# Queries and keys in one transfer of 112 partitions, one row of values, keys and gates, token rows in order of making, list entries of 64 bytes

## The chip, the core and the metric

The program runs on one core of a Trainium2 chip. Its engines are TensorE (PE, with its weight loads PEld), VectorE (DVE), ScalarE (ACT), GpSimd (POOL) and SyncE (SP, which here only issues transfers). Transfers are issued from the queues of SP, ACT and POOL and carried by 16 DMA engines. The metric is the time of one execution on the device in microseconds (us), the median of the runs.

## The reference

Two stages in a row: a recurrent memory with exponential gates over 4 sequences of 8 heads, 768 steps and 40 columns a head, and then a layer of 16 experts, in 4 groups of 4, to which each of the 3072 tokens is routed alone. Cut to what matters:

```python
for t in range(S):                                   # S = 768, B = 4, H = 8, D = 40
    m_new = np.maximum(f_gate[:, :, t] + m, i_gate[:, :, t])
    f_stab = np.exp(f_gate[:, :, t] + m - m_new)
    i_stab = np.exp(i_gate[:, :, t] - m_new)
    m = m_new
    C = f_stab * C + i_stab * outer(vt, kt)
    n = f_stab * n + i_stab * kt
    y[:, :, t] = sigmoid(o_gate[:, :, t]) * (C @ qt) / np.maximum(np.abs(n @ qt), 1.0)
x = y.transpose(0, 2, 1, 3).reshape(B * S, H * D)    # 3072 tokens of 320
g_idx = argmax(x @ w_group); e_idx = argmax(x @ w_expert[g_idx])
out[token] = g_w * e_w * (np.maximum(x @ w1[g, e], 0) @ w2[g, e])   # 320 -> 1024 -> 320
```

## The kernel before

**Attention.** The sequence is cut into 12 chunks of 64 steps, and the 4 sequences into 2 pairs, so that there are 24 units `u`. A unit's 128 partitions are 64 steps of two sequences. `unit(u)` is written out by hand as a row of stages: `scores` (PE, products of keys and queries), `masked` (DVE, `pt`, the scores times the decays `ab`), `carried` (PE, the state of earlier chunks), `state` (PE), `decayed` (POOL), `carried2` (DVE), `values` (PE), `busy` (products that are thrown away), `decay(u + 2)` (PE `aw`, then eight exponentials on ACT, `ab`), `norm`, `state2` (DVE), `keyw(u + 1)` (POOL), `turn(u - 1)`, `norm1`, `rows` and `rows2`. `rows` makes `xn` from the sums and the output gates, `rows2` makes the token rows `x` (on POOL up to unit 19, on DVE after). `turn` copies 64 columns (ACT), stores the rows to the DRAM tensor `x_d`, and turns them on PE (`tp`, then the ACT copy `xT`) for the router. The tile `x` has three buffers.

**Loads.** `unit(u)` starts with `loads(u + 3)`: queries and keys `qk` (four buffers) in two transfers of 48 partitions, at partitions 0 and 64, and `nt` (four buffers), values and keys by row. The output gates come as `sig` for four units at once, and one tanh on ACT (`gate_o`) covers four units.

**Routing.** Every fourth unit, `logits_of` takes four units' `xT` to logits on PE, copies them on ACT (`lT`) and turns them back on PE. `route` is a list of small DVE steps that are put in between the units one at a time (`go_on`): the choice of group and expert, the place of each token in its expert's list (`slot`), and its factor `cb`, which is stored behind its row in `x_d` (columns 384 to 391). `put_id` writes the tokens' numbers into the lists `itab` in DRAM, 128 at a time, by an indirect DMA from POOL. The lists are filled beforehand with the number of a dummy row (`first_tokens`).

**Experts.** When the counts of the first five sixths of the tokens are known, the two fullest experts are picked and their weights loaded. The first 256 tokens of the fullest one (`(0, 0)`) are gathered while the last four units still run, the next 128 (`(0, 1)`) come by the late list `li`, when the last unit's `slot` is written; then come the other 15 experts. Weights are split into a high and a low part (`w1h`, `w1l`, `wsk`, `w2h`, `w2l`: the high parts on ACT, the low parts on DVE), tokens into `xhl`; `psh` and `hh` are the hidden layer, `po` and `y` the output, which an indirect DMA scatters to the tokens' rows. `ix` are list pieces read back, `xg` the gathered rows.

**Order.** Up to unit 21 instructions go out in the order in which they are written. From unit 22 on a scheduler orders them by its own estimates, and each engine and each queue then runs its own in that order. A transfer on SP's queue that has to wait for its data holds up every transfer behind it.

Of the kernel before, what the change touches and what calls it, by code (L numbers as in the profile page):

```python
# [18 lines left out]
P = 128  # L19
# [19 lines left out]
QR = 48  # L39
# [22 lines left out]
def lstm_moe(ctx: ExitStack, tc: tile.TileContext, gates, qkT, nat, og, wcat, w1, w2, cst, out):  # L62
# [7 lines left out]
    itab = dram.tile([NE * NBLK + 1, P], I32, name="itab")  # L70
    itab_flat = itab.rearrange("a (p o) -> (a p) o", o=1)
# [11 lines left out]
    tokid = const.tile([P, NU], I32, name="tokid")  # L83
# [217 lines left out]
    def x_rows(c, p):  # L301
        return [x_d[(NP * p + b) * S + c * L:(NP * p + b) * S + (c + 1) * L] for b in range(2)]

    def turn(u):
        x = st_[u]["x"]
        nc.scalar.copy(x[:, DM:3 * P], x[:, 2 * P:DM])
        done = [nc.sync.dma_start(rows_[:, 0:3 * P], x[halves(b)]) for b, rows_ in enumerate(x_rows(*divmod(u, NP)))]
        if u // 4 == NG - 1:
            no_order("early", *done)
# [30 lines left out]
    def logits_of(c, n):  # L340
# [7 lines left out]
        nc.scalar.copy(lT[0:32 * n], t[0:32 * n])  # L348
        nc.tensor.transpose(out=bank[:, 0:32 * n], in_=lT[0:32 * n], identity=ident[0:32 * n, 0:32 * n])
# [4 lines left out]
    def route(c, b0, b1, bank):  # L354
# [54 lines left out]
        ids.extend((slot[:, b - b0:b - b0 + 1], tokid[:, c * 4 + b:c * 4 + b + 1]) for b in range(b0, b1))  # L409
# [38 lines left out]
    def no_order(key, *some):  # L448

        for ins in some:  # L450
            for o in unordered.setdefault(key, []):
                tc.declare_no_dep(ins.ins, o.ins, reason="distinct rows")
        unordered[key].extend(some)


    def first_rows():
        t = wst.tile([P, 3 * F], F32, name="w1s")
        none, zero = t[:, 0:NE * NBLK].bitcast(I32), t[:, F:F + ROW]
        nc.gpsimd.memset(none, DUMMY)
        nc.gpsimd.memset(zero, 0.0)  # L460
        rt["rows"] = none, zero

    def first_tokens():
        none = rt["rows"][0]
        nc.sync.dma_start(itab[0:NE * NBLK, :].rearrange("(p a) b -> p (a b)", p=P), none)
        nc.sync.dma_start(itab[NE * NBLK:NE * NBLK + 1, :], none[0:1, 0:P])

    def last_rows():
        zero = rt["rows"][1]
        for b in range(B):  # L470
            nc.sync.dma_start(x_d[b * S + S - P:(b + 1) * S, :], zero)
        nc.sync.dma_start(x_d[NTOK:NTOK + 1, :], zero[0:1])
# [127 lines left out]
    def load_ix(r, q=None):  # L600
        nb = len(blocks(CAPS[r]))
        ixs[r] = mxp.tile([P, 3], I32, name="ix", bufs=5)
        t = itab[0:NE * NBLK].rearrange("(e n) p -> e n p", e=NE)
        (q or nc.sync).dma_start(ixs[r][:, 0:nb], t[bass.ds(ereg[r], 1), 0:nb, :].rearrange("o n p -> p (o n)"))
# [4 lines left out]
    def load_x(W, idx, early=False):  # L609
        xg = []  # L610
        for i, m in enumerate(blocks(W)):
            g = mxp.tile([P, ROW], F32, name="xg", bufs=9)
            ins = gather(g, x_d, idx(i, P))
# [66 lines left out]
    def expert(key, W, ws, xg, idx, between=(), then=None, last=None):  # L680
# [65 lines left out]
        for i, m in enumerate(blocks(W)):  # L746
# [27 lines left out]
            done = scatter(y[0:m], idx(i, m))  # L774
# [16 lines left out]
    def ix_of(r):  # L791
        return lambda i, m: ixs[r][0:m, i:i + 1]
# [4 lines left out]
    def unit(u):  # L797
# [5 lines left out]
        if u % 4 == 1 and u // 4 + 1 < NG:  # L803
            load_o(u // 4 + 1)
# [8 lines left out]
        run(carried2, u)  # L813
        go_on()
# [5 lines left out]
        if u % 4 == 1 and 1 < u < NU - 4:  # L820
            logits_of(u // 4 - 1, 4)
        if u == NU - 4:
            logits_of(NG - 2, 3)
# [14 lines left out]
        if u % 4 == 3 and u // 4 + 1 < NG:  # L838
            gate_o(u // 4 + 1)
# [54 lines left out]
    with tc.manual_schedule():  # L894
# [18 lines left out]
        load_o(0)  # L913
# [31 lines left out]
        nc.gpsimd.tensor_copy(tokid, cs[:, C_TOK:C_TOK + NU])  # L945
# [62 lines left out]
    for r in range(NEARLY):  # L1008
        li = mxp.tile([P, 1], I32, name="li", bufs=2)
        nc.sync.dma_start(li, itab_flat[bass.ds(lreg, P), :])  # L1010
        late_ix[r] = lambda i, m, t=li: t[0:m, 0:1]
# [38 lines left out]
    with tc.For_i(0, nv, 1):  # L1050
# [23 lines left out]
        ix = wk2.tile([P, 1], I32, name="ix1")  # L1074
        gather(ix, itab_flat, si)
        g = mxp.tile([P, ROW], F32, name="xg", bufs=9)
        gather(g, x_d, ix)
# [21 lines left out]
        scatter(y, ix)  # L1099
# [5 lines left out]
def _lay(inputs):  # L1105
# [6 lines left out]
    def tr(a):  # L1112
        a = a.reshape(NP, 2, 2, 4, NCH, L, D).transpose(4, 0, 2, 6, 3, 1, 5).reshape(NU, 2, D, 4, P)
        return np.concatenate([a, np.zeros_like(a[:, :, :QR - D])], axis=2)

    qkT = c(np.stack([tr(k), tr(q)], axis=3))
# [8 lines left out]
    nat = c(np.concatenate([vv.reshape(NU, P, DM + H), rows_s(k).reshape(NU, P, DM)], axis=-1))  # L1125
    og = c(rows(o).reshape(NU, P, DM).transpose(1, 0, 2))
# [29 lines left out]
    return {'gates': gates, 'qkT': qkT, 'nat': nat, 'og': og, 'wcat': wcat, 'w1': w1, 'w2': w2, 'cst': cst}  # L1156
# [22 lines left out]
```

## Time and profile before

| | us |
|---|---|
| median of 3 runs | 475.73 |
| lowest, highest | 473.14, 479.25 |
| the profiled execution | 477.46 |
| its span, first to last instruction | 475.4 |

| engine | busy us | share of the span |
|---|---|---|
| PE | 407.7 | 86% |
| PEld | 364.6 | 77% |
| DVE | 284.9 | 60% |
| ACT | 216.5 | 46% |
| POOL | 170.0 | 36% |

The shares are means over two stages with different limits, attention up to some 200 us and experts after it; so the stretches are read apart. A row of a timeline says when an instruction (or several alike in a row, x2) started, how long it took, and in brackets how long its engine had stood idle before it and what ended that. On SP's queue the time is that of issuing the transfer, not of the transfer.

### The profile page before, as it was taken

The page shows a single profiled execution, that of the slowest core. Times are in us where ns is not written, and L with a number is a line of the kernel's source. Part 1 is how long each engine was busy: PE and PEld are TensorE (multiplying, and loading weights), DVE is VectorE, ACT ScalarE, POOL GpSimd, SP SyncE. Part 2 cuts the span into 40 slices and gives each one's busy share as a digit, 9 for nine tenths or more (in the row PEclk, how much of TensorE's full clock was granted, in tenths as well). Part 3 has the DMA queues.
Part 4 walks back from the last instruction along what each step waited for, and adds up shares of the span by engine and source line. Part 5 has one row for each costly group of instructions (what it writes and reads, how often), then busy time and mean ns, then how long its engine had stood idle before and what let it go on. Part 6 is the DMA issues. An engine that isn't in the chain of part 4 may idle for free.

```text
span 475.4 us, 13522 instructions
## 1 busy us (share of the span) xinstructions
PE 407.7 (86%) x5470; PEld 364.6 (77%) x5470; DVE 284.9 (60%) x718; ACT 216.5 (46%) x549; POOL 170.0 (36%) x209
## 2 busy tenths in 40 slices
PE   5667986977854878689399999999999999999995
PEld 3355864665643656568399999999999999999995
DVE  5477465575833777362667475485667677777331
ACT  1524244244413533016077454575565665567421
POOL 4234346354541543230543504432331265133210
PEclk8666698579775755559799999999999999999998
DMA  8933478987399535438589635758665876654300
GB/s 212 238 94 91 112 213 160 237 159 192 70 198 310 71 96 146 92 121 185 124 278 418 216 129 196 254 181 292 215 218 194 288 278 215 223 183 143 147 15 9
DMA packets 30227, 85.74 MB, mean 180 GB/s; under 512 B 12961, under 2 KB 16746, under 8 KB 26580
## 3 DMA queue, kind: packets, MB, share of 16 engines
q1 hardware_dynamic: 24788, 67.63, 50.6%
q0 software_dynamic: 5152, 16.75, 9.9%
q8 instruction: 43, 0.70, 0.7%
q10 hardware_dynamic: 224, 0.49, 0.4%
q14 instruction: 20, 0.16, 0.1%
HBM read 75.08 MB, written 10.62 MB: 180 GB/s over the span
## 4 chain that ended last, share of the span: by engine, by line
PE 62%; issue 10%; DMA 9%; DVE 9%; ACT 3%; SPq 3%; POOL 2%; POOLq 1%; ACTq 0%; DVEq 0%
PE psh L736 17%; PE po L759 6%; PE po L757 5%; PE po L758 5%; PE busy L131 4%; PE X L260 3%; PE X L196 3%; ACT ab L181 3%; PE tpm L298 3%; PE Y L236 2%; DMA w1s<-in_w_dram 2%; DMA ix<-itab 2%; PE po L763 2%; PE Y L220 2%; PE po L762 2%
## 5 line engine op out<-in xcount | busy, mean ns | idle before, releaser
L181 ACT ACTIVATE ab<-aw,bcol 128x64 f32<-128x64 f32 x192 | 41.8, 332 | 84.7 <-PE aw L178 80.1
L759 PE MATMUL po<-w2h,hh 128*128 128x320 f32 (+1 forms) x208 | 64.8, 312 | 8.4 <-DVE hh L693 8.4
L571 POOL DMA_INDIRECT xg<-x_d,ix x34 | 39.2, 1154 | 81.4 <-DMA ix<-itab 27.4
L575 POOL DMA_INDIRECT out_dram<-y,ix x34 | 41.6, 1225 | 72.0 <-ACT y L769 58.4
L757 PE MATMUL po<-w2h,hh 128*128 128x320 f32 (+1 forms) x208 | 66.2, 319 | 0.0
L758 PE MATMUL po<-w2l,hh 128*128 128x320 f32 (+1 forms) x208 | 64.6, 311 | 0.0
L633 DVE TENSOR_TENSOR w2l<-w2s,w2h 128x640 fp32r<-128x640 f32 x64 | 50.3, 823 | 20.1 <-ACT w2h L631 20.1
L736 PE MATMUL psh<-xhl,w1h 128*128 128x256 f32 (+4 forms) x352 | 60.0, 292 | 1.0 <-DVE slot L408 0.5
L736 PEld LDWEIGHTS psh<-xhl,w1h 128*128 128x128 f32 x352 | 51.0, 194 | 1.5 <-DVE slot L408 0.8
L693 DVE SCALAR_TENSOR_TENSOR hh<-psh,hh 128x256 fp32r<-128x256 f32 (+2 forms) x104 | 39.6, 412 | 17.3 <-ACT hh L690 16.7
L690 ACT ACTIVATE hh<-psh 128x512 fp32r<-128x512 f32 (+5 forms) x68 | 33.3, 490 | 35.1 <-PE psh L736 26.3
L759 PEld LDWEIGHTS po<-w2h,hh 128*128 128x128 f32 (+1 forms) x208 | 39.4, 190 | 8.6 <-DVE hh L693 8.6
L633 DVE TENSOR_TENSOR w1l<-w1s,w1h 128x1024 fp32r<-128x1024 f32 x26 | 31.7, 1221 | 19.6 <-DMA ix<-itab 8.5
L631 ACT CAST w2h<-w2s 128x640 fp32r<-128x640 f32 x64 | 43.0, 725 | 0.0
L757 PEld LDWEIGHTS po<-w2h,hh 128*128 128x128 f32 (+1 forms) x208 | 39.3, 189 | 0.1
L758 PEld LDWEIGHTS po<-w2l,hh 128*128 128x128 f32 (+1 forms) x208 | 39.3, 189 | 0.0
L769 ACT ACTIVATE y<-po,xg 128x320 f32<-128x320 f32 (+1 forms) x26 | 13.7, 528 | 52.3 <-PE po L759 50.1
L131 PE MATMUL busy<-ones_b 128*128 128x512 bf16 x85 | 35.5, 550 | 2.2 <-DVE sep L899 1.2
L736 PE MATMUL psh<-xhl,w1l 128*128 128x256 f32 (+4 forms) x176 | 36.8, 291 | 0.0
L736 PE MATMUL psh<-xhl,wsk 128*128 128x256 f32 (+4 forms) x176 | 36.7, 291 | 0.0
L260 PE MATMUL X<-nt,pt 64*64 64x41 f32 x768 | 22.1, 268 | 16.3 <-DVE pt L202 11.3
L478 POOL DMA_INDIRECT itab<-tokid,slot x24 | 24.9, 1039 | 26.5 <-DVE slot L408 12.8
(192 smaller groups left out, 867.3 us busy)
## 6 DMA issues: line engine op xcount, KB each, us to landing
w1s<-in_w_dram SPq DMA_DIRECT2D x12, 1536.0 KB, 7.4
w2s<-in_w_dram SPq DMA_DIRECT2D x12, 1280.0 KB, 6.0
qk<-in_qkT_dram SPq DMA_DIRECT2D x48, 192.0 KB, 6.0
nt<-in_nat_dram SPq DMA_DIRECT2D x24, 324.0 KB, 5.7
x_d<-x SPq DMA_DIRECT2D x48, 96.0 KB, 4.2
sig<-in_og_dram SPq DMA_DIRECT2D x6, 640.0 KB, 8.3
w1s<-in_w_dram SPq DMA_DIRECT2D x4, 768.0 KB, 9.4
w1s<-in_w_dram POOLq DMA_DIRECT2D x2, 1536.0 KB, 7.4
```

The source lines that it names most:

```text
L131: mm(t, ones_b, bc(ones_b.unsqueeze(1), (P, 4, P)), start=True, stop=True)
L181: rt["exp"] = nc.scalar.activation(ab[:, i, :], aw[:, i, :], AF.Exp, bias=bcol[:, u, i:i + 1])
L260: mm(X[halves(b), a, cols_of(2 * r + m, base=4 * L)], t["pt"][halves(a), r, cols_of(k, L)], t["nt"][halves(a), cols_of(4 * r + k)], start= ...
L571: return nc.gpsimd.indirect_dma_start(out=o, out_offset=None, in_=src, in_offset=bass.IndirectOffsetOnAxis(ap=idx, axis=0))
L575: return nc.gpsimd.indirect_dma_start(out=out, out_offset=bass.IndirectOffsetOnAxis(ap=idx, axis=0), in_=y, in_offset=None, bounds_check=N ...
L631: nc.scalar.copy(a, src[:, s])
L633: lows.append(lambda: nc.vector.tensor_tensor(o[rows], src[rows, s], a[rows].bitcast(F32), op=ALU.subtract))
L693: nc.vector.scalar_tensor_tensor(hh[:, f:f + per, dst], src[:, :, t], 0.0, hr.bitcast(F32)[:, :, t], op0=ALU.max, op1=ALU.subtract)
L736: ins = mm(ps[:, g * W:(g + 1) * W], w[:, s], x, start=(n == 0), stop=(n == len(todo) - 1))
L757: mm(po[0:m], hh[:, f, t], w2h[:, s], start=st0, stop=False)
L758: mm(po[0:m], hh[:, f, t], w2l[:, s], start=False, stop=False)
L759: ins = mm(po[0:m], hh[:, f, tl], w2h[:, s], start=False, stop=sp0)
```

## The change

- `qk` comes in one transfer of 112 partitions; the 16 in between are zeros.
- The output gates are columns of `nt` (976 columns for 648), so `sig` and its transfers go, and `gate_o` is one tanh of 320 columns in every unit, after `scores`.
- `x_d` holds its rows in order of making (unit, partition) and no longer by token: a unit's rows are stored by one transfer of 128 partitions for two of 64, and a group's `cb` by one for four.
- A list entry is 64 bytes for 4: the row's number and the token's, eight times. The row's number serves the gathers, the token's the scatter of the output. Only the first three blocks of each list are filled beforehand, by two transfers.
- `logits_of` is cut in two: products and the copy `lT` come before `values`, the turning back where it was.

```diff
-QR = 48
+QR = 112
+WIDE = 16
+NAT = 976
+K0, O0 = DM + H, 2 * DM + H
...
-    itab = dram.tile([NE * NBLK + 1, P], I32, name="itab")
-    itab_flat = itab.rearrange("a (p o) -> (a p) o", o=1)
+    itab = dram.tile([NE * NBLK + 1, P, WIDE], I32, name="itab")
+    itab_flat = itab.rearrange("a p o -> (a p) o")
...
-        for r in range(2):
-            nc.sync.dma_start(qk[64 * r:64 * r + QR], qkT[u, r])
+        nc.sync.dma_start(qk[0:QR], qkT[u])
...
-    def gate_o(c):
-        nc.scalar.activation(sigs[c], sigs[c], AF.Tanh, scale=0.5)
+    def gate_o(u):
+        o = st_[u]["nt"][:, O0:O0 + DM]
+        nc.scalar.activation(o, o, AF.Tanh, scale=0.5)
...
-        nt = natp.tile([P, 2 * DM + H], F32, name="nt")
+        nt = natp.tile([P, NAT], F32, name="nt")
...
-        done = [nc.sync.dma_start(rows_[:, 0:3 * P], x[halves(b)]) for b, rows_ in enumerate(x_rows(*divmod(u, NP)))]
+        ins = nc.sync.dma_start(x_d[u * P:(u + 1) * P, 0:3 * P], x)
...
-        for b in range(2):
-            xv = x_d[0:NTOK].rearrange("(p b c t) r -> b t c p r", p=NP, b=2, c=NCH)[b, :, 2 * c:2 * c + 2, :, 3 * P:ROW]
-            for i in range(b0 // NP, (b1 + 1) // NP):
-                lo, hi = max(b0, i * NP), min(b1, (i + 1) * NP)
-                nc.sync.dma_start(xv[:, i, lo - i * NP:hi - i * NP, :], cb[halves(b), lo - b0:hi - b0, :])
+        xv = x_d[0:NTOK].rearrange("(u p) r -> p u r", p=P)
+        nc.sync.dma_start(xv[:, 4 * c + b0:4 * c + b1, 3 * P:ROW], cb)
...
-        nc.gpsimd.memset(none, DUMMY)
+        nc.gpsimd.memset(none[0:NE], DUMMY)
...
-        nc.sync.dma_start(itab[0:NE * NBLK, :].rearrange("(p a) b -> p (a b)", p=P), none)
+        t = itab[0:NE * NBLK].rearrange("(e n) p o -> e (n p o)", e=NE)
+        n = 3 * P * WIDE // 2
+        for k in range(2):
+            nc.sync.dma_start(t[:, k * n:(k + 1) * n], none[0:NE, 0:n])
...
-        ixs[r] = mxp.tile([P, 3], I32, name="ix", bufs=5)
+        ixs[r] = mxp.tile([P, 3, 2], I32, name="ix", bufs=5)
...
             run(scores, u)
+        run(gate_o, u)
...
+        parts = ()
+        if u % 4 == 1 and 1 < u < NU - 4:
+            parts = [lambda f=f: f(u // 4 - 1, 4) for f in (logits_of, logits_at)]
...
+        for f in parts[:1]:
+            f()
         go_on()
         run(values, u)
...
-        if u % 4 == 1 and 1 < u < NU - 4:
-            logits_of(u // 4 - 1, 4)
...
+        for f in parts[1:]:
+            f()
...
-        nc.gpsimd.tensor_copy(tokid, cs[:, C_TOK:C_TOK + NU])
+        nc.gpsimd.iota(tokid[:, :, :, 0], pattern=[[P, NU], [0, WIDE // 2]], base=0, channel_multiplier=1)
+        nc.gpsimd.tensor_copy(tokid[:, :, :, 1], bc(cs[:, C_TOK:C_TOK + NU].unsqueeze(2), (P, NU, WIDE // 2)))
```

The scheduler and the shorter rows of transfers also move instructions. Three places follow. In each, the names are those of the tiles and tensors, and the sizes partitions by columns.

SP's queue around the loads of the last unit, unit 23 (`qk_91` and the `nt` behind it), before:

```order
L589 DMA w2s<-in_w_dram 128x1280
L150 DMA qk_90<-in_qkT_dram 48x1024 x2
L167 DMA nt<-in_nat_dram 128x648
L435 DMA x_d<-cb 64x2x8
L435 DMA x_d<-cb 64x8
L435 DMA x_d<-cb 64x2x8
L435 DMA x_d<-cb 64x8
L307 DMA x_d<-x 64x384 x2
L589 ISA
L589 DMA w1s<-in_w_dram 128x1536
L150 DMA qk_91<-in_qkT_dram 48x1024 x2
L167 DMA nt<-in_nat_dram 128x648
```

and after:

```order
L584 DMA w2s<-in_w_dram 128x1280
L152 DMA qk_90<-in_qkT_dram 112x1024
L163 DMA nt<-in_nat_dram 128x976
L299 DMA x_d<-x 128x384
L584 ISA
L584 DMA w1s<-in_w_dram 128x1536
L152 DMA qk_91<-in_qkT_dram 112x1024
L163 DMA nt<-in_nat_dram 128x976
L428 DMA x_d<-cb 128x4x8
L299 DMA x_d<-x 128x384
L584 ISA
L584 DMA w1s<-in_w_dram 128x1536
```

The four stores of `cb` that stood ahead of unit 23's loads are gone from there; one store of `cb` stands behind them.

SP's queue from the last units' stores to the late list `li`, before:

```order
L589 DMA w2s<-in_w_dram 128x1280
L435 DMA x_d<-cb 64x2x8
L435 DMA x_d<-cb 64x8
L435 DMA x_d<-cb 64x2x8
L435 DMA x_d<-cb 64x8 x3
L589 ISA
L589 DMA w2s<-in_w_dram 128x1280
L307 DMA x_d<-x 64x384 x4
L1006 TENSOR_LOAD late_i
L1010 REGISTER_ALU
L1010 DMA li<-itab 128x1
```

and after:

```order
L584 DMA w2s<-in_w_dram 128x1280
L299 DMA x_d<-x 128x384
L584 ISA
L584 DMA w2s<-in_w_dram 128x1280
L428 DMA x_d<-cb 128x8
L299 DMA x_d<-x 128x384 x2
L428 DMA x_d<-cb 128x3x8
L428 DMA x_d<-cb 128x8
L1003 TENSOR_LOAD late_i
L1007 ISA
L1007 DMA li<-itab 128x2
```

The rows of the last two units (`x4` before, `x2` after) are now stored ahead of the last group's `cb`, not behind it and a weight load. On POOL's queue, at the same place, before:

```order
L478 DMA itab<-tokid,slot 49280x1 x4
L581 TENSOR_LOAD ewi
L589 ISA
L589 DMA w1s<-in_w_dram 128x3072
L581 TENSOR_LOAD ewi
L571 DMA xg<-x_d,li 128x392
L571 DMA xg<-x_d,ix 128x392 x3
```

and after:

```order
L473 DMA itab<-tokid,slot 49280x16 x4
L566 DMA xg<-x_d,li 128x392
L566 DMA xg<-x_d,ix 128x392
L576 TENSOR_LOAD ewi
L566 DMA xg<-x_d,ix 128x392 x2
L584 ISA
L584 DMA w1s<-in_w_dram 128x3072
```

The weights of the third expert (`w1s` here) were issued ahead of the gathers and now stand behind them.

ACT where the first expert begins, after the last exponentials of the router, before:

```order
L675 CAST xhl<-tpm 128x3x128 x2
L690 ACTIVATE hh<-psh 128x2x256 x3
L631 CAST w1h<-w1s 128x1024 x2
L631 CAST wsk<-w1s 128x1024
L690 ACTIVATE hh<-psh 128x2x256
L631 CAST w2h<-w2s 128x640 x4
```

and after:

```order
L626 CAST w1h<-w1s 128x1024
L670 CAST xhl<-tpm 128x3x128 x2
L626 CAST w1h<-w1s 128x1024
L626 CAST wsk<-w1s 128x1024
L626 CAST w2h<-w2s 128x640 x4
L685 ACTIVATE hh<-psh 128x2x256 x4
```

and DVE at the same place, before:

```order
L566 TENSOR_REDUCE tot_f<-ovr 128x1
L567 CAST total<-tot_f 128x1
L693 SCALAR_TENSOR_TENSOR hh<-psh,hh 128x2x256 x3
L633 TENSOR_TENSOR w1l<-w1s,w1h 128x1024 x2
L633 TENSOR_TENSOR wsk<-w1s,wsk 64x1024
L693 SCALAR_TENSOR_TENSOR hh<-psh,hh 128x2x256
```

and after:

```order
L404 CAST slot<-slf 128x1
L628 TENSOR_TENSOR w1l<-w1s,w1h 128x1024
L671 TENSOR_TENSOR xhl<-tpm,xhl 128x3x128 x2
L533 TENSOR_REDUCE pos<-big 128x16
L628 TENSOR_TENSOR w1l<-w1s,w1h 128x1024
L537 TENSOR_TENSOR sel<-pos,cs 128x32
```

The split of the second expert's weights has moved ahead of the first expert's `hh` on both engines, and its first piece ahead of `xhl`.

## Rows read from the trace of the kernel before

**Rows 1.** Stretches: attention, handover, experts; busy us (instructions) by engine, clock, DMA.

```profile
22.00:185.00 163.00, 124.68 (x3316) 97.87 (x3317) 99.69 (x301) 61.77 (x237) 66.68 (x97) 0.71 0.66 153
185.00:238.00 53.00, 37.30 (x275) 31.97 (x276) 28.47 (x112) 11.93 (x24) 18.18 (x25) 0.64 0.55 139
238.00:475.40 237.40, 231.88 (x1722) 227.79 (x1720) 146.49 (x278) 134.78 (x260) 77.83 (x68) 0.99 0.58 204
```

**Rows 2.** Timeline of DVE, 150 to 236 us.

```profile
183.00 0.69 DVE L202 TENSOR_TENSOR pt<-X,ab 128x512 f32<-128x512 f32 x1 [3.01 <-PE X L196]
...
193.15 0.69 DVE L202 TENSOR_TENSOR pt<-X,ab 128x512 f32<-128x512 f32 x1 [2.25 <-PE X L196]
...
196.27 0.20 DVE L281 RECIPROCAL den<-den 128x8 f32<-128x8 f32 x1
...
199.31 0.49 DVE L292 TENSOR_TENSOR x<-xn,den 128x320 f32<-128x320 f32 x1 [0.24 <-DMA x_d<-x]
...
210.57 0.14 DVE L408 CAST slot<-slf 128x1 int32<-128x1 f32 x1
...
228.69 2.36 DVE L633 TENSOR_TENSOR w1l<-w1s,w1h 128x1024 fp32r<-128x1024 f32 x2 [8.51 <-DMA ix<-itab]
```

**Rows 3.** Timeline of SP's queue, 145 to 245 us: issues.

```profile
177.28 2.59 SPq L435 DMA_DIRECT2D x_d<-cb  x4
...
182.67 0.83 SPq L150 DMA_DIRECT2D qk<-in_qkT_dram  x2
...
194.76 4.12 SPq L307 DMA_DIRECT2D x_d<-x  x6
...
208.35 3.84 SPq L435 DMA_DIRECT2D x_d<-cb  x6
...
214.33 2.54 SPq L307 DMA_DIRECT2D x_d<-x  x4
```

**Rows 4.** Timeline of PE, 224 to 239 us.

```profile
233.14 0.63 PE L759 MATMUL po<-w2h,hh 128*128 128x320 f32 x1 [8.38 <-DVE hh L693]
...
238.04 0.28 PE L715 MATMUL psh<-xhl,w1h 128*128 128x256 f32 x1
```

**Rows 5.** The chain of work that ended last: start, us, what.

```profile
134.26 8.61 DMA w1s<-in_w_dram
...
212.72 7.07 DMA itab<-tokid,slot
...
220.37 8.35 DMA ix<-itab
```

**Rows 6.** Timeline of POOL, 205 to 240 us.

```profile
214.21 0.57 POOL L589 DMA_DIRECT2D w1s<-in_w_dram  x1 [0.53 <-DVE cntr L554]
229.54 1.26 POOL L571 DMA_INDIRECT xg<-x_d,li  x1 [14.76 <-DMA ix<-itab]
```

**Rows 7.** Waits of PE, 22 to 185 us: total us, times, longest.

```profile
PE lg L349 <- ACT lT L348: 9.9, 5, 6.4
PE X L260 <- issue: 4.9, 3, 2.9
```

**Rows 8.** Timeline of SP's queue, 100 to 150 us.

```profile
125.14 4.04 SPq L435 DMA_DIRECT2D x_d<-cb  x4
```

**Rows 9.** The page's transfer issues: times issued, KB each, median us to landing.

```profile
qk<-in_qkT_dram SPq DMA_DIRECT2D x48, 192.0 KB, 6.0
nt<-in_nat_dram SPq DMA_DIRECT2D x24, 324.0 KB, 5.7
...
out_dram<-y,ix POOLq DMA_INDIRECT x34, 5.2
itab<-tokid,slot POOLq DMA_INDIRECT x24, 6.1
```

**Rows 10.** Groups of POOL, 0 to 240 us, by form: busy us, mean ns.

```profile
L459 POOL MEMSET w1s<- 128x384 int32 x1 | 0.4, 417 | 0.0
```

**Rows 11.** Timeline of ACT, 236 to 275 us.

```profile
243.21 1.05 ACT L631 CAST w1h<-w1s 128x1024 fp32r<-128x1024 f32 x1
```

More of the change, by code (lines that the diff above doesn't have):

```diff
@@ L61, in lstm_moe @@
 @with_exitstack
-def lstm_moe(ctx: ExitStack, tc: tile.TileContext, gates, qkT, nat, og, wcat, w1, w2, cst, out):
+def lstm_moe(ctx: ExitStack, tc: tile.TileContext, gates, qkT, nat, wcat, w1, w2, cst, out):
     nc = tc.nc
@@ L306, in turn @@
         nc.scalar.copy(x[:, DM:3 * P], x[:, 2 * P:DM])
-        done = [nc.sync.dma_start(rows_[:, 0:3 * P], x[halves(b)]) for b, rows_ in enumerate(x_rows(*divmod(u, NP)))]
+        ins = nc.sync.dma_start(x_d[u * P:(u + 1) * P, 0:3 * P], x)
         if u // 4 == NG - 1:
-            no_order("early", *done)
+            no_order("early", ins)
         tp = ps_1.tile([P, 3, P], F32, name="tp", tag="tp")
@@ L408, in route @@
         rt["last"] = nc.vector.tensor_copy(slot, slf)
-        ids.extend((slot[:, b - b0:b - b0 + 1], tokid[:, c * 4 + b:c * 4 + b + 1]) for b in range(b0, b1))
+        ids.extend((slot[:, b - b0:b - b0 + 1], tokid[:, c * 4 + b].rearrange("p a o -> p (a o)")) for b in range(b0, b1))
         yield
@@ L446, in lstm_moe, with no_order @@
     unordered = {}
[L448 to L453, printed above, removed]
+    def no_order(key, ins):
+        for o in unordered.setdefault(key, []):
+            tc.declare_no_dep(ins.ins, o.ins, reason="distinct rows")
+        unordered[key].append(ins)
     def first_rows():
-        t = wst.tile([P, 3 * F], F32, name="w1s")
-        none, zero = t[:, 0:NE * NBLK].bitcast(I32), t[:, F:F + ROW]
-        nc.gpsimd.memset(none, DUMMY)
+        none = wst.tile([P, 3 * F], F32, name="w1s").bitcast(I32)
+        zero = wst.tile([P, NF * DM], F32, name="w2s")[:, 0:ROW]
+        nc.gpsimd.memset(none[0:NE], DUMMY)
         nc.gpsimd.memset(zero, 0.0)
@@ L612, in load_x @@
             g = mxp.tile([P, ROW], F32, name="xg", bufs=9)
-            ins = gather(g, x_d, idx(i, P))
+            ins = gather(g, x_d, idx(i, P, 0))
             if early:
@@ L773, in expert @@
                 nc.vector.tensor_scalar(y[0:m], y[0:m], comb, None, op0=ALU.mult)
-            done = scatter(y[0:m], idx(i, m))
+            done = scatter(y[0:m], idx(i, m, 1))
             no_order("out", done)
@@ L813, in unit @@
         run(carried2, u)
+        parts = ()
+        if u % 4 == 1 and 1 < u < NU - 4:
+            parts = [lambda f=f: f(u // 4 - 1, 4) for f in (logits_of, logits_at)]
+        if u == NU - 4:
+            parts = [lambda f=f: f(NG - 2, 3) for f in (logits_of, logits_at)]
+        for f in parts[:1]:
+            f()
         go_on()
@@ L912, in lstm_moe @@
         loads(1)
-        load_o(0)
         loads(2)
@@ L1073, in lstm_moe @@
         nc.vector.tensor_scalar(si, sl, float(NSLOT), None, op0=ALU.add)
-        ix = wk2.tile([P, 1], I32, name="ix1")
+        ix = wk2.tile([P, WIDE], I32, name="ix1")
         gather(ix, itab_flat, si)
         g = mxp.tile([P, ROW], F32, name="xg", bufs=9)
-        gather(g, x_d, ix)
+        gather(g, x_d, ix[:, 0:1])
         w1s = wst.tile([P, 3 * F], F32, name="w1s")
@@ L1098, in lstm_moe @@
         nc.vector.tensor_scalar(y, po, g[:, 3 * P:3 * P + 1], None, op0=ALU.mult)
-        scatter(y, ix)
+        scatter(y, ix[:, 1:2])
 _OUTS = [((NTOK, DM), 'float32')]
@@ L1112, in tr @@
     def tr(a):
-        a = a.reshape(NP, 2, 2, 4, NCH, L, D).transpose(4, 0, 2, 6, 3, 1, 5).reshape(NU, 2, D, 4, P)
-        return np.concatenate([a, np.zeros_like(a[:, :, :QR - D])], axis=2)
-    qkT = c(np.stack([tr(k), tr(q)], axis=3))
+        return a.reshape(NP, 2, 2, 4, NCH, L, D).transpose(4, 0, 2, 6, 3, 1, 5).reshape(NU, 2, D, 4, P)
+    qkT = np.zeros((NU, QR, 2, 4, P), np.float32)
+    for r in range(2):
+        for i, a in enumerate((k, q)):
+            qkT[:, 64 * r:64 * r + D, i] = tr(a)[:, r]
     def rows(a):
@@ L1124, in _lay @@
     vv = np.concatenate([rows_s(v), np.ones((NU, P, H, 1), v.dtype)], axis=-1)
-    nat = c(np.concatenate([vv.reshape(NU, P, DM + H), rows_s(k).reshape(NU, P, DM)], axis=-1))
-    og = c(rows(o).reshape(NU, P, DM).transpose(1, 0, 2))
+    nat = np.zeros((NU, P, NAT), np.float32)
+    for i, a in ((0, vv), (K0, rows_s(k)), (O0, rows(o))):
+        nat[:, :, i:i + a[0, 0].size] = a.reshape(NU, P, -1)
     wg, we = inputs['moe_w_group'], inputs['moe_w_expert']
```

43 lines of the change are left out of this document (16 added, 27 removed).

## The prediction, made before the changed kernel ran

> **What bounds the kernel now.** First the stretches [rows 1]. From 238 us to the end PE is busy 231.9 of 237.4 us at a granted clock of 0.99, so at the upper of its two levels (2.4 GHz): the experts are bound by products that the change does not touch. From 22 to 185 us (attention) PE is busy 124.7 of 163 us at a mean clock of 0.71, ACT 61.8 and POOL 66.7, and the DMA engines 0.66 of the time: no engine is full, and a unit takes as long as its chain of waits. From 185 to 238 us, the handover, PE is busy 37.3 of 53 us at 0.64. A change in the order of loads and stores can only pay in the first two.
>
> Then the handover, by DVE's timeline [rows 2] against SP's queue [rows 3]. Unit 22's masked scores start at 183.00 us, unit 23's only at 193.15, after a wait of 2.25 us for PE: the products needed `qk` of unit 23, issued at 182.67 us behind four stores of `cb` (177.28, 2.59 us), and a `qk` takes 6.0 us to land [rows 9]. Unit 23's token rows start at 199.31 us, though their divisor was done at 196.47: `x` has three buffers, unit 19's was still being stored, and that store was one of the six issued from 194.76 us on. The last `slot` is done at 210.57 us. The stores of units 22 and 23 went out only at 214.33 us, behind the last `cb` (208.35). DVE stood 8.51 us before `w1l` at 228.69 us. The view names a list read as what ended it; `w1l` is laid over the tiles of attention, so I read it as waiting for those last stores. Behind `w1l` in DVE's order stood the first expert's last `hh`, and PE stood 8.38 us for that, until 233.14 us [rows 4]. Beside this runs the list path: the last write to the lists was issued at 212.72 us and took 7.07 us, the read of `li` and `ix` 8.35 us [rows 5], with the third expert's `w1s`, 1.5 MB, issued among it at 214.21 us; the gather by `li` starts at 229.54 us [rows 6], and the products of `(0, 1)` at 238.04 us [rows 4].
>
> **Attention, part by part.** (1) SP's queue. A group's `cb` costs 4.04 us of issuing just ahead of the first expert's `w1s` [rows 8]; that `w1s` is a link of the chain for 8.61 us [rows 5], since ACT waits for it with the exponentials behind. One transfer with the same number of pieces should cost between 1.0 us (a quarter) and 4.0 us (if issuing goes by pieces); I take 2.0. The second `qk` and the second `x` save some 0.4 and 0.6 us (0.83 for two and 4.12 for six, [rows 3]). So `w1s` comes 3.0 us earlier (0 to 4.6).
>
> (2) The router's copy. PE stood 9.9 us in five places for `lT`, 6.4 of it at one [rows 7]; that one is the place of (1). In the other four it was 3.5 us, because `lT` stood behind eight exponentials. Now it stands ahead of them and the products ahead of `values`. I take off 3.5 us (0 to 5).
>
> (3) The lists' filling. The memset has 384 columns in 417 ns [rows 10]; 3072 columns are at most eight times that, 3.3 us, so POOL is held 2.9 us longer once, and 392 KB are then written for 192. POOL is idle 96 of 163 us, so most of it is covered; where it isn't, the first list write and the decay of the state behind it are late. I put on 0.5 us (0 to 4).
>
> (4) The tanh. Six of 1280 columns become 24 of 320. None can cost more than the 1.05 us that ACT takes for 1024 columns [rows 11], 25 us in all at the very most, and ACT is idle 101 of 163 us, waiting for `aw`, which is where they stand. Zero (0 to 2).
>
> (5) The transfers themselves. Per unit 384 + 324 + 160 KB become 448 + 488: 8% more bytes in fewer transfers, with the DMA engines at 0.66. Zero (a loss of 2 to the gain of the first rival). That `nt` is now held until `xn` costs nothing while SP reaches the next `nt` after the previous unit's `x` anyway. Together: 3.0 + 3.5 - 0.5 = 6.0 us off.
>
> On (5) a row and a rule can be weighed. `qk` takes 6.0 us to land with 192 KB, `nt` 5.7 with 324 KB [rows 9]: partition count, not bytes, seems to set it. The Trainium skill ("SBUF — State Buffer", Door 1: the DMA port swizzle) says that 64 partitions of one half reach only 8 of 16 ports, 196 GB/s against 328 for all 128, and that two transfers to the two halves do not add up. By it a pair of `qk`, 2.0 us at the ports, would become some 1.4 us, an estimate from that page; the rows agree in sign.
>
> **The handover.** All places are on the clock of the kernel before. (6) Unit 23's loads are issued ahead of `cb`, up to 5.4 us earlier (182.67 - 177.28), so its wait of 2.25 us goes: -2.3 (0 to 5.4). (7) Unit 19's store no longer stands behind six `cb`, so the rows need not wait from 196.47 to 199.31: -2.8. Unit 22's turning and logits then no longer stand between unit 23's rows and its `slot`, 10.8 us apart now; of those I take 2 (0 to 5). So `slot` comes at 210.6 - 7.1 = 203.5 us.
>
> (8) PE's path. The last stores go out ahead of the last `cb`, and `w1l` ahead of `hh` no longer waits: -8.4. ACT now does six casts before the first `hh`, some 5 us at 1.05 us for 1024 columns, while PE makes its first products; I take that as covered, up to 2.5 if not. By this path `(0, 1)` could start at 238.0 - 7.1 - 8.4 = 222.5 us.
>
> (9) The list path took 19.0 us from `slot` to the gather (229.54 - 210.57). The read of 8.35 us loses its neighbour `w1s`, which is now issued behind the gathers: I take 4 off (0, if the pieces set it, to 5). The write: a list write takes 6.1 us to land, a scatter of the output's rows, 1280 bytes each, 5.2 [rows 9]; 64 bytes for 4 may get that difference: 1 off (0 to 2). So the gather at 203.5 + 14.0 = 217.5 us, and the products 5 to 8.5 us later (8.5 now): 222.5 to 226, say 224.
>
> The Trainium skill speaks against a gain at the write ("DMA: Bandwidth & Descriptors", Specifications): below 512 bytes a write is a read-modify-write, and 64 is still below. By it the 1 us falls away and the sum is 1 us longer; no row here has both sizes.
>
> (10) What is late next: the third expert's `w1s`, now behind four gathers of some 1.3 us, so at 222.7 us, landing at 231 (8.35 as above). ACT wants it 5.2 us after the first products of `(0, 1)` (243.21 against 238.04), at 229.2, and has `hh` and `xhl` behind it. So some 2 us are given back. The handover ends 14 - 1 = 13 us earlier (I count half, since PE still has products in hand).
>
> **Sum.** The profiled execution took 477.46 us (475.4 of span and 2.1 around it; 1.7 above the median shown). 477.5 - 6.0 - 13 = 458.5; I forecast 458 us.
>
> **Rivals.**
> *The transfers are the bound, and fewer ports make them so.* Then every unit gets shorter, not only the named places. For it: the difference in landing, and the stops of PE inside a row of products that the profile puts to "issue", 4.9 us at `values` alone [rows 7], with the DMA engines at 0.66. Against it: 0.66 is not 1, and bytes grow. If these stops and as much again in the other stages go, it is 10 us less: 448 us. By the rule of the Trainium skill on ports, above, this is what would follow.
>
> *The list takes the place of the stores.* For it: the list path and PE's path are only 1.5 us apart in my own sum, and reads of 4 or 8 bytes a piece stay as many. If the read keeps its 8.35 us and the write its 7.07, (9) gives nothing: the gather at 222.4, products at 229 to 231, the gain of (8) hidden; 238 - 230 = 8, so 477.5 - 6 - 8 = 463.5, and with half of (1) and (2) 467. Against it: the neighbour `w1s` is really moved.
>
> *Not faster: the first `hh` waits for weights.* ACT's four `w2h` of the second expert now stand ahead of the first `hh`. If their last half lands as late as the late stores did (228.7 us), the first `hh` comes at some 231.5 instead of the 214 that PE's products allow, and `(0, 1)` starts some 13.5 us after it, at 245: 7 us later, so 477.5 + 7 - 6 = 478.5. It decides from the point at which that half lands after some 209 us. Against it: it is issued right behind unit 21's rows, about 20 us earlier than that needs.
>
> **How the numbers follow.** My forecast, 452 to 463, gets 0.57, the first rival 0.15, the second 0.23, the third 0.05. The range leaves out the third and the outer ends: 446 to 468. A measurement of this kernel tells about 2% from no change, so faster means below 466.2 us: all of the forecast and the first rival and half of the second, 0.83. Within 2%: 0.13. Slower: 0.04.
>
> **What would show it.** (6) `pt` of the last two units some 8 us apart or less. (7) No DVE wait for a store before `x`. (8) No stop of PE inside the first expert's `po`. (9) `li` and `ix` landing in 4 to 5 us, list writes in about 5. (10) ACT standing before the third expert's `w1h` for 2 us or less. (1) `w1s` of the first expert issued near 131 us. (2) No PE wait for `lT`. The prediction is wrong if the experts' stretch, from the products of `(0, 1)` to the end, is not 237 us again, or if attention loses time by late `nt` or `qk`.

## The result and the profile after

The changed kernel takes 456.44 us (median of four executions, 451.54 to 459.49) where the kernel before, beside it, takes 475.67: a ratio of 0.9556, with a 95% interval of 0.9449 to 0.9663. The forecast was 458 us, 446 to 468. Ratios leave out slow executions, those more than 1.5% above the fastest of their kernel (here the one of 459.49), so they differ somewhat from the ratio of the medians. One execution of the changed kernel differs from the next by up to 8 us, and the profiled one (449.6 us of span) is the shortest; so single profiles are compared below by stretches, and kernels by their ratio to the kernel before that ran beside them.

The stretches of the changed kernel, cut at the same events as [rows 1] (columns: window and its length, then busy us and instructions of PE, PEld, DVE, ACT, POOL, the granted clock, the DMA engines' share, GB/s):

```profile
22.00:173.70 151.70, 119.65 (x3328) 93.43 (x3326) 103.29 (x310) 65.00 (x257) 72.02 (x102) 0.78 0.65 193
173.70:211.20 37.50, 32.24 (x261) 28.47 (x262) 24.23 (x99) 11.51 (x21) 16.93 (x23) 0.73 0.45 140
211.20:449.60 238.40, 232.06 (x1722) 227.75 (x1720) 146.64 (x278) 134.99 (x260) 77.08 (x67) 1.00 0.59 203
```

Attention is 11.3 us shorter (163.0 to 151.7), the handover 15.5 (53.0 to 37.5), and the experts are 1.0 longer. In attention the DMA engines are busy for the same share as before, 0.65 for 0.66, but they move 193 GB/s for 153. That pair of numbers is what I had not read.

DVE's timeline of the changed kernel, the rows that answer to [rows 2]:

```profile
171.73 0.68 DVE L198 TENSOR_TENSOR pt<-X,ab 128x512 f32<-128x512 f32 x1
...
179.21 0.69 DVE L198 TENSOR_TENSOR pt<-X,ab 128x512 f32<-128x512 f32 x1 [1.70 <-PE X L192]
...
184.35 0.55 DVE L287 TENSOR_TENSOR x<-xn,den 128x320 f32<-128x320 f32 x1
...
192.48 0.15 DVE L404 CAST slot<-slf 128x1 int32<-128x1 f32 x1
192.55 1.23 DVE L628 TENSOR_TENSOR w1l<-w1s,w1h 128x1024 fp32r<-128x1024 f32 x1
```

The last two `pt` are 7.5 us apart for 10.2, `x` waits for no store, the last `slot` comes 13.3 us behind the last `pt` for 17.4, and `w1l` waits for nothing.

SP's queue, as [rows 3]:

```profile
175.34 0.32 SPq L428 DMA_DIRECT2D x_d<-cb  x1
180.93 4.64 SPq L299 DMA_DIRECT2D x_d<-x  x2
188.01 2.71 SPq L428 DMA_DIRECT2D x_d<-cb  x2
195.76 0.34 SPq L1007 DMA_DIRECT2D li<-itab  x1
```

POOL's queue: the last list write and the gather by the late list, as [rows 5] and [rows 6]:

```profile
192.96 1.65 POOL L473 DMA_INDIRECT itab<-tokid,slot  x1 [0.30 <-DVE slot L404]
199.12 0.98 POOL L566 DMA_INDIRECT xg<-x_d,li  x1 [4.51 <-DMA ix<-itab]
```

The list path, `slot` to gather, takes 6.6 us for 19.0: the read of `li` follows the last list write after 2.8 us (7.1 before), and the gather follows that read after 3.4 (9.7).

PE's timeline, as [rows 4], the first product of `(0, 1)`:

```profile
211.19 0.28 PE L710 MATMUL psh<-xhl,w1h 128*128 128x256 f32 x1
```

From 194.76 us on PE goes through the first expert without a stop of a microsecond, so PE's path ends the handover, and the gathered rows lie ready.

### The profile page after: what moved, and what is told of

Same layout as the page of the kernel before. It is cut to its first block, busy times and chain, and to the rows that moved or that the text cites. A ratio compares the mean times of both kernels' runs of the same rounds, so it can differ in the third digit from the quotient of the medians.

```text
span 449.6 us, 13434 instructions
## 1 busy us (share of the span) xinstructions
PE 398.5 (89%) x5470; PEld 357.0 (79%) x5470; DVE 285.0 (63%) x718; ACT 218.8 (49%) x567; POOL 173.7 (39%) x210
## 4 chain that ended last, share of the span: by engine, by line
PE 68%; DVE 13%; issue 10%; ACT 3%; POOL 2%; DMA 2%; POOLq 1%; DVEq 0%
PE psh L731 20%; PE po L752 6%; PE po L754 6%; PE po L753 6%; PE busy L134 4%; PE X L256 4%; ACT ab L177 2%; PE tpm L293 2%; PE po L758 2%; PE X L192 2%; PE po L757 2%; PE psh L699 1%; PE Y L232 1%; PE Y L216 1%; DVE pt L198 1%
## 5 line engine op out<-in xcount | busy, mean ns | idle before, releaser
L566 POOL DMA_INDIRECT xg<-x_d,ix x34 | 41.2, 1210 | 82.7 <-DMA ix<-itab 37.6
L570 POOL DMA_INDIRECT out_dram<-y,ix x34 | 39.7, 1168 | 76.3 <-ACT y L764 62.1
L752 PEld LDWEIGHTS po<-w2h,hh 128*128 128x128 f32 (+1 forms) x208 | 38.9, 187 | 0.1
L754 PEld LDWEIGHTS po<-w2h,hh 128*128 128x128 f32 (+1 forms) x208 | 38.8, 187 | 0.0
L287 POOL TENSOR_TENSOR x<-xn,den 128x320 f32<-128x320 f32 x20 | 16.4, 818 | 49.3 <-DVE xn L282 47.2
```

What stands on the lines that cost most here:

```text
L566: return nc.gpsimd.indirect_dma_start(out=o, out_offset=None, in_=src, in_offset=bass.IndirectOffsetOnAxis(ap=idx, axis=0))
L570: return nc.gpsimd.indirect_dma_start(out=out, out_offset=bass.IndirectOffsetOnAxis(ap=idx, axis=0), in_=y, in_offset=None, bounds_check=N ...
L752: mm(po[0:m], hh[:, f, t], w2h[:, s], start=st0, stop=False)
L754: ins = mm(po[0:m], hh[:, f, tl], w2h[:, s], start=False, stop=sp0)
```

## The experiments

Each kernel was timed beside the kernel before, whose median was 476.9 to 480.5 us beside these runs; so the ratios can be compared, the times only roughly. "The changed kernel" is also run a second time, since it varies. The edits are shown in part; `...` marks lines that are left out.

**again**: no edit.

> The changed kernel a second time, unchanged, for a second profile beside which the edits of this group are read. Expected 455 to 458 us, a ratio to before of 0.955 to 0.963. Its profiled execution was 451.5, the lowest of four; if a usual execution differs from it by one stretch (attention, the handover or the experts), the second profile shows which: by my account attention, since the first profile's attention is 11.3 us shorter than before's where I had summed 6.0, and its experts' stretch is the same as before's.

Measured: 0.9483 (0.936 to 0.9606), 456.77 us: the time as expected, the ratio lower. Its profile (457.4 us of span) has nearly the same handover from the last `pt` on and the same experts: `(0, 1)` comes 32.3 us behind the last `pt` (32.0 in the first profile), the experts take 238.3. The last `pt` is 7.6 us later, so all of the difference lies before it, 4.2 us of it from unit 20's `pt` to unit 23's. The last section says what differs there.

**entries8**: list entries short again.

```diff
-WIDE = 16
+WIDE = 2
```

> The changed kernel with list entries of 8 bytes (one number of a row and one of a token) for 64; the order on every engine and queue stays. From the last slot to the gather by the late list it takes 6.6 us in the changed kernel and took 19.0 before. Theory A (the transfers issued around the list path and ahead of it on its queue made it long, the size of an entry gives about 1 us at the write): 7 to 9 us here, behind PE's path, which ends at 211 us while the gather starts at 199: no change, within 1.5 us of the changed kernel's. Theory B (the size of the entry did it): 15 to 19 us, the gather at 208 to 211, the products of the late block 4 to 8 us later, some 462 us.

Measured: 0.9793 (0.9727 to 0.9858), 468.72 us: 12 us of the gain are gone, and theory A with them. But they are not lost where theory B looked. The late block is as far behind the last `pt` as in the changed kernel (32.6 us), and the list path takes 9.3 us. It is attention that is as long as before. DVE's timeline, the last two units:

```profile
185.00 0.69 DVE L198 TENSOR_TENSOR pt<-X,ab 128x512 f32<-128x512 f32 x1 [0.96 <-PE X L192]
...
195.35 0.69 DVE L198 TENSOR_TENSOR pt<-X,ab 128x512 f32<-128x512 f32 x1 [4.20 <-PE X L192]
```

Before they were at 183.00 and 193.15 us [rows 2]. What does it? The stretch from 171 to 179 us (a weight transfer of the second expert, behind list writes) of entries8:

```profile
171.00:179.00 8.00, 6.50 (x119) 5.57 (x114) 5.67 (x24) 2.44 (x7) 0.76 (x2) 0.50 1.04 127
```

Here the DMA engines count as busy all the time (1.04) and move 127 GB/s. Where the entries are long, such a share moves more than twice as much: 1.04 goes with 300 GB/s in a row of `again` below. The kernel before has such stretches too; two of them, 81 to 84 us and the 7 us behind its last list writes:

```profile
81.00:84.00 3.00, 0.99 (x29) 0.76 (x23) 0.37 (x1) 0.00 (x0) 0.87 (x2) 0.82 1.03 97
213.00:220.00 7.00, 7.00 (x50) 7.00 (x49) 4.10 (x15) 2.34 (x4) 1.25 (x2) 0.78 0.75 48
```

All fourteen traces of this case agree with this. Cut into stretches of 3 us from 20 to 250 us, the rate at a share above 0.9 falls to 42 GB/s in the kernel before and to 52 in entries8; in the twelve profiles with entries of 32 or 64 bytes it is never below 166. The stores of `cb`, 32 bytes a piece, stand just ahead of some of these stretches too, but they are in the other kernels as well. So transfers in flight crawl behind writes of 4 or 8 bytes: theory C of the next runs.

**before_wide**: the kernel before with long entries (the token sixteen times) and what goes with them, the lists' filling and their reads.

```diff
+WIDE = 16
...
-    itab = dram.tile([NE * NBLK + 1, P], I32, name="itab")
-    itab_flat = itab.rearrange("a (p o) -> (a p) o", o=1)
+    itab = dram.tile([NE * NBLK + 1, P, WIDE], I32, name="itab")
+    itab_flat = itab.rearrange("a p o -> (a p) o")
...
-    tokid = const.tile([P, NU], I32, name="tokid")
+    tokid = const.tile([P, NU, WIDE], I32, name="tokid")
...
```

> The kernel before with list entries of 64 bytes (the token sixteen times) for 4, and nothing else: the order on every engine and queue is that of before, the lists' filling is as in the changed kernel. Theory C (a list write of 4 or 8 bytes a piece makes the transfers behind it crawl, so that w1s, nt and qk land late): the first expert's w1s lands in 4 to 6 us for 8.6, unit 23's pt comes at 182 to 187 us for 193, the 7 us between the last list write and the read of li become 3; the tail behind unit 23's pt stays at some 40 us, since the order is that of before; 463 to 467 us. Theory A (queue order and fewer issues): no more than 1 us at the list write, and the memset 0.5 us the other way, 474 to 477 us.

Measured: 0.9758 (0.9713 to 0.9804), 464.86 us, as theory C had it: 12 us from the entries alone, with the instructions in the order of before (the lists' filling apart). Its issue rows (times issued, median us to landing) give a list write 3.0 us for the 6.1 of [rows 9] (3.4, 3.8 and 4.3 in the other profiles with long entries that have the figure: two_qk, token_rows and rows64):

```profile
itab<-tokid,slot POOLq DMA_INDIRECT x24, 3.0
```

The stretch behind its last list writes, where before moved 48 GB/s:

```profile
206.00:213.00 7.00, 7.00 (x55) 7.00 (x54) 3.10 (x10) 3.58 (x6) 0.54 (x1) 0.87 0.97 312
```

The waits that I had put down to order shrink with it. PE's waits for `lT` in attention (total, times, longest), 9.9, 5 and 6.4 in [rows 7]:

```profile
PE lg L350 <- ACT lT L349: 4.4, 5, 1.2
```

And DVE's and PE's stops in the first expert, 8.51 and 8.38 us in [rows 2, 4]:

```profile
186.36 0.69 DVE L203 TENSOR_TENSOR pt<-X,ab 128x512 f32<-128x512 f32 x1 [2.54 <-PE X L197]
...
215.33 2.36 DVE L637 TENSOR_TENSOR w1l<-w1s,w1h 128x1024 fp32r<-128x1024 f32 x2 [3.39 <-DMA ix<-itab]
```

```profile
219.77 0.41 PE L763 MATMUL po<-w2h,hh 128*128 128x320 f32 x1 [3.25 <-DVE hh L697]
...
223.18 0.38 PE L719 MATMUL psh<-xhl,w1h 128*128 128x256 f32 x1
```

The last `pt` is 6.8 us earlier than before, and `(0, 1)` 36.8 us behind it for 44.9. The order of before still costs its 10.4 us between the last two `pt`, and 3.3 us at `hh`.

**entries32**: the changed kernel with entries of 32 bytes.

```diff
-WIDE = 16
+WIDE = 8
```

> The changed kernel with list entries of 32 bytes for 64; the order on every engine stays. If what holds the transfers behind a list write up is that a piece is shorter than 64 bytes, it is as slow as with 8 bytes: 464 to 469 us. If the cost falls with every byte: some 461. If 32 bytes are long enough: 455 to 458 us.

Measured: 0.9454 (0.9393 to 0.9515), 454.94 us. 32 bytes are as good as 64; the harm of 4 and 8 ends somewhere between 8 and 32. Longer entries than 64 bytes were not run, so it is not shown that 32 and 64 cost nothing.

**rows64**: `cb` written in 64 bytes.

```diff
-ROW = 3 * P + 8
+ROW = 3 * P + 16
...
-        cb = post.tile([P, n, 8], F32, name="cb")
+        cb = post.tile([P, n, 16], F32, name="cb")
...
```

> The changed kernel with a token row of 400 columns (1600 bytes) for 392 and its factor written in 64 bytes for 32, in the same order on every engine. If theory C holds for every short write, and not for those of the lists alone, the stores of cb hold the transfers behind them up too: 450 to 454 us, with the packets behind the stores at 167 and 175 us no slower than elsewhere. If 32 bytes from an even address are long enough, or a store of SP's queue is another matter than an indirect one: no change, 455 to 458.

Measured: 0.9451 (0.9406 to 0.9496), 451.09 us. The time lies in the range of the first theory, but the interval overlaps those of the changed kernel's two runs, and two_qk_rows64 (below) shows no gain from the same edit, so none is claimed. That fits entries32, where 32 bytes were as good as 64.

**gates_apart**: the output gates again as one transfer and one tanh for four units.

```diff
...
+        t = wk.tile([P, B, DM], F32, name="sig")
+        nc.sync.dma_start(t, nat[c * B:(c + 1) * B, :, O0:O0 + DM].rearrange("u p d -> p u d"))
...
-        nt = natp.tile([P, NAT], F32, name="nt")
-        nc.sync.dma_start(nt, nat[u])
+        nt = natp.tile([P, O0], F32, name="nt")
+        nc.sync.dma_start(nt, nat[u, :, 0:O0])
...
```

> The changed kernel with the output gates again in one transfer and one tanh for four units (nt with 648 columns). The first expert's w1s waits 1.65 us on ACT in the changed kernel and waited 8.6 before. Theory A (the four stores of cb ahead of it on SP's queue made it late, 3 us, and its landing takes as long as it did): ACT's wait stays under 4 us, and the time within 2 us. Theory B (the 640 KB of sig, issued just then, share the engines with it): its landing takes 8 us again, ACT stands 4 to 6 us more before w1h, units 18 and 19 are later by as much, 460 to 462 us. If the tanh of 24 pieces cost something after all, the units without it are each some 0.2 us shorter.

Measured: 0.9563 (0.9494 to 0.9633), 457.3 us: no difference that can be told. ACT waits 0.4 us in all for the first expert's `w1s`. My theory B was wrong about the place, too: `sig` is issued at 137.83 us, behind both pieces of `w1s` (130.89 and 136.42), so it could not make them late.

**token_rows**: token rows in the tokens' order, two stores a unit and four of `cb`.

```diff
-        ins = nc.sync.dma_start(x_d[u * P:(u + 1) * P, 0:3 * P], x)
+        done = [nc.sync.dma_start(rows_[:, 0:3 * P], x[halves(b)]) for b, rows_ in enumerate(x_rows(*divmod(u, NP)))]
...
```

> The changed kernel with the token rows again in the tokens' order: two stores of 64 partitions a unit and four of cb a group, entries of 64 bytes kept. Theory A (handover: unit 23's loads behind cb 2.3 us, the x buffer 2.8, the last stores behind the last cb and before w1l 8.4): some 8 to 13 us later behind unit 21, and 2 us at the first w1s; 466 to 470 us. Theory C (all the rest is the list entries): attention up to unit 21 as in the changed kernel, and the handover no more than 3 us longer, 457 to 460 us.

Measured: 0.9529 (0.9461 to 0.9598), 455.03 us. Undoing the rows' order costs nothing that can be told. The scheduler goes back to much of the old order, and the stops are small: DVE's and PE's rows of this kernel.

```profile
207.56 2.36 DVE L635 TENSOR_TENSOR w1l<-w1s,w1h 128x1024 fp32r<-128x1024 f32 x2 [2.58 <-DMA ix<-itab]
```

```profile
212.00 0.41 PE L761 MATMUL po<-w2h,hh 128*128 128x320 f32 x1 [2.44 <-DVE hh L695]
```

**split_late**: the second expert's splits held back behind the first expert's last `hh`.

```diff
...
-    with tc.issue_after(rt["last"].ins):
+    with tc.issue_after(rt["act00"].ins):
         do(split, 3)
```

(`act00` is the last relu of `(0, 0)`.)

> The changed kernel with the casts and differences of the second expert's weights held back behind the first expert's last hh on ACT and DVE. Theory A (what was worth 8.4 us is only that w1l does not wait for late stores): w1l waits for nothing that is late, and the time is the same to 2 us more, since the second expert's w1h then comes some 5 us later than now. Theory B (that the second expert's weights are split ahead of the first expert's hh is itself the gain): PE stands before the second expert's products for 5 us or more, 461 to 465 us.

Measured: 0.945 (0.938 to 0.952), 451.24 us; `(0, 1)` 32.5 us behind the last `pt`. Theory A: that these casts go first is no gain in itself. Its median is lower than the changed kernel's, but the intervals overlap.

**two_qk**: queries and keys in two transfers of 48 partitions, out of the same tensor.

```diff
-        nc.sync.dma_start(qk[0:QR], qkT[u])
+        for r in range(2):
+            nc.sync.dma_start(qk[64 * r:64 * r + 48], qkT[u, 64 * r:64 * r + 48])
```

> The changed kernel with queries and keys again in two transfers of 48 partitions; at the handover the scheduler then puts the hh of the first expert ahead of the second expert's w1h and w1l again, and a weight transfer ahead of the gathers. Theory A (the pair costs 0.4 us of issuing a unit, hidden but for the places where SP is late): up to unit 21 no more than 1 us later; behind it the order of split_late, which cost nothing: 456 to 459 us. Theory D (64 partitions use fewer ports, so every unit's transfers take longer): units 3 to 21 later by 5 us and more, 462 to 466 us.

Measured: 0.9337 (0.9279 to 0.9395), 446.35 us; only two_qk_rows64 (below) has as low a ratio. Both theories are wrong, and theory D has the sign wrong: by the times, the edit in the change's own name costs something. Since the scheduler's order at the handover changes with it, two runs divide it.

**two_early** and **two_late**: two transfers for units 0 to 17 alone (the order at the handover stays), and for units 18 to 23 alone (the order is that of two_qk; its edit has `u >= 18` for `u < 18`).

```diff
-        nc.sync.dma_start(qk[0:QR], qkT[u])
+        if u < 18:
+            for r in range(2):
+                nc.sync.dma_start(qk[64 * r:64 * r + 48], qkT[u, 64 * r:64 * r + 48])
+        else:
+            nc.sync.dma_start(qk[0:QR], qkT[u])
```

> The changed kernel with queries and keys in two transfers of 48 partitions for units 0 to 17 alone, one transfer of 112 after; the order at the handover stays that of the changed kernel (ACT's last exp stands two places later). With all units in two transfers the time was 446.35 us for some 456.6 in the changed kernel, and the scheduler's order at the handover was another. Theory E (one transfer of 112 partitions is itself the dearer one in attention): 447 to 450 us. Theory F (the order at the handover is what paid): 454 to 457 us.

> The changed kernel with queries and keys in two transfers for units 18 to 23 alone; the order on SP, ACT and DVE at the handover is then that of the kernel with two transfers everywhere. Theory E (one transfer of 112 partitions is the dearer one in attention): 451 to 455 us, the gain of the last quarter alone. Theory F (the order at the handover: the first expert's xhl and hh ahead of the second expert's w1l): 446 to 449 us, with the products of the late block 30.6 us behind unit 23's pt for the 32 of the changed kernel, and more of it in the units before.

Measured: two_early 0.9357 (0.9302 to 0.9412), 450.12 us, and two_late 0.9422 (0.9368 to 0.9477), 452.58 us, where the kernel before took 480.04 beside them. With the order kept, two_early has two_qk's ratio within the noise, so that ratio does not need the other order: as theory E has it. two_late decides nothing, since its interval overlaps that of two_qk and that of `again`. The profiles do not show where in attention the time is won: unit 20's `pt` starts at 157.2 us in two_early and 158.0 in two_qk, with one transfer at 156.9 (split_late), 157.6 (rows64) and up to 162.9 (`again`). So theory E rests on the times alone. The order itself is small: `(0, 1)` is 32.1 us behind the last `pt` in two_early and 30.5 in two_late.

**two_qk_rows64**: both edits.

> The changed kernel with queries and keys in two transfers and a token row of 400 columns with its factor written in 64 bytes: what the two runs before point to. If both are gains of their own: 440 to 444 us. If the one with 400 columns was no more than chance: 445 to 448 us.

Measured: 0.9334 (0.9266 to 0.9403), 451.22 us: the ratio of two_qk.

## Why the prediction was right, and where it was not

The time came out as forecast; half of the reasons did not.

**The handover was right in its sum and in most of its parts.** (6) Unit 23's `pt` is 7.5 us behind unit 22's (8.5 in `again`), 2.7 less (2.3 forecast). It is 10.4 in before_wide, which has the old order, and 10.4 in entries8 too, which has the new one with short entries: the new order alone, the reason that (6) gives, does not bring it. (7) From the last `pt` to `slot` it takes 4.2 us less (4.8 forecast), in entries8 too. (The rows that waited for unit 19's store were unit 22's, 2.11 us until 198.58; unit 23's stood behind them on DVE. The price is the same.) (8) PE's stop for `hh` is gone (8.4); entries8, with the new order and short entries, has no such stop either, so the order is enough for it. (10) The third expert's `w1s` is not waited for, so the reason was wrong; that the experts' stretch is 1.0 us longer, as counted, is chance. In all the handover gave 15.5 less 1.0, where 14 less 1 stood in the sum.

**What ends the handover was put down too narrowly in (8).** I read `w1l` as waiting for late stores. The trace of before bears that out as far as it goes: two of the four stores of `x` issued from 214.33 us have a landing in it, 12.3 and 13.0 us after their issue, where the median of all such stores is 4.2. But 5.1 of the 8.4 us are also gone in before_wide, where the order is that of before: much of the lateness came from the crawl. Order and entries each remove most of the same stop, so the two gains do not add up there: `(0, 1)` comes 44.9 us behind the last `pt` in the kernel before, 36.8 with the entries alone, 32.6 with all but the entries and 32.0 with both.

**(9) was mis-sized.** The write was given 1 us for its size, from 6.1 against 5.2. It takes 3.0 by the entry alone. The list path lost 12.3 us for the 5 forecast, and the read, which was given 4 for its neighbour `w1s`, gave more than the write: in entries8 the path is 9.3 us, so the order took 9.7 us off with entries still short. There the gather follows the read after 3.1 us (9.7 before), and the read follows the last write after 5.7 (7.1 before, 2.8 with long entries). PE's path ends later, so the second rival (the list takes over) did not come; nor did the third, since the first `hh` waits for no weights.

**(5) is the step that failed.** "The transfers themselves: zero" came from a DMA share of 0.66. entries8 and before_wide show that the gain of attention sits there: with short entries and every other part of the change, the last `pt` is at 195.35 us (193.15 before); with long entries alone at 186.36, with both at 179.21 and 186.83 in the two profiles. The landing of `w1s` (1) and the wait for `lT` (2) were real waits, 8.6 and 9.9 us. In entries8 the second is gone and the first halved (4.2), and attention is no shorter. The 6.5 us of (1) and (2) stood in the sum for a cause that I had not seen; attention lost 4.6 and 11.3 us in the two profiles. That the total agrees is luck in this part.

**(3) and (4) were right.** The memset took 2.6 us, once, and nothing waits for it. gates_apart shows no cost of the tanh.

**The rule against (9) did not decide.** The prediction cited the Trainium skill ("DMA: Bandwidth & Descriptors", Specifications) for a limit of 512 bytes, below which a write is a read-modify-write, so that 64 bytes are on the same side of it as 4. The runs show a step that this limit does not have: entries of 32 bytes are as good as 64, and 4 and 8 cost some 12 us. Entries of 512 bytes or more were not run, so the limit itself is not tested.

**The first rival fell, and with its sign.** The transfers did bound attention, but by the crawl; that ports did is not shown. One transfer of 112 partitions seems slower than two of 48, by some 1 to 2% of the kernel: the ratio is 0.934, 0.936 and 0.933 in two_qk, two_early and two_qk_rows64, and 0.945 to 0.956 in the seven runs that have long entries, the rest of the change or most of it, and one transfer. Some of the intervals overlap, and no profile shows the place. The Trainium skill ("SBUF — State Buffer", Door 1) would have it the other way; no run here shows that gain.

**What stays open.** Why the single `qk` would be dearer: it carries 448 KB for 384 of which the difference is zeros, and it was not tried with fewer rows. And whether the harm of 4 and 8 bytes comes from the length of a piece, or from neighbours being written by different DMA engines: entries of 4 bytes lie side by side in a list, and short entries at a wide spacing were not run. The split of `logits_of` was not undone alone: PE's waits for `lT` are 9.9 us before, 4.4 in before_wide and none in the changed kernel, but what that is worth in time is not shown.

## What to carry to other kernels

Read the DMA engines' share and their GB/s together: a share near 1 at a third of the usual rate is not a load but a crawl, and what was issued just ahead of it is the suspect, to be confirmed by an edit of that alone. A scatter of short pieces is paid for by the transfers behind it: here long list entries alone were worth as much (0.976) as all the rest of the change without them (0.979). When one change has several parts, undo each alone: here one part gave the gain of attention, two gave nothing that can be told once the entries were long, and one seems to have taken 1 to 2% back.

## What the runs showed of the hardware

The changed kernel's two profiles differ by 7.8 us, and a part of that goes with TensorE's clock. In the first one unit 20's `values` wait 0.32 us for `pt`, and the stretches from 160 to 180 us are granted 1.00 and 0.72 (the column after the engines):

```profile
160.29 0.68 PE L256 MATMUL X<-nt,pt 64*64 64x41 f32 x32 [0.32 <-DVE pt L198]
```

```profile
160.00:170.00 10.00, 8.23 (x259) 6.71 (x261) 9.18 (x39) 7.08 (x27) 4.14 (x8) 1.00 0.91 269
170.00:180.00 10.00, 7.39 (x142) 6.16 (x133) 7.38 (x36) 1.56 (x5) 5.34 (x11) 0.72 0.57 178
```

In `again` PE stands 2.96 us for the same `pt`, until 163.65 us, and is then granted the lower level (1.2 of 2.4 GHz):

```profile
163.65 1.09 PE L256 MATMUL X<-nt,pt 64*64 64x41 f32 x32 [2.96 <-DVE pt L198]
```

```profile
160.00:170.00 10.00, 7.04 (x157) 5.56 (x151) 7.19 (x18) 3.70 (x15) 6.29 (x8) 0.63 1.04 300
170.00:180.00 10.00, 9.07 (x150) 7.16 (x150) 7.68 (x33) 4.96 (x17) 2.81 (x7) 0.50 0.62 185
```

The row of 32 products of `values` takes 1.09 us for 0.68, and from unit 20's `pt` to unit 23's it takes 23.9 us for 19.7. It is not only this execution: two_early has a stop of 2.95 us at the same product, 0.50 in both stretches and 24.2 us. The level is not all of it: two_qk is granted 1.00 from 160 to 165 us and 0.53 and 0.50 in the next two stretches of 5 us, and takes 20.1 us. So in attention, one late `pt` may cost more by the clock than by its own wait; this is argued from a few profiles, and no run changed the clock alone.
